# A fused attention and feed-forward kernel: a stored order of its pieces in place of a planner that orders them while the kernel is built

## The chip, the cores and the metric

The kernel runs on one core of one Trainium2 chip. The metric is device time in microseconds (us), taken over several runs; a verdict compares runs of two kernels on the same chip. The timed figure of a run is 1.7 to 2.1 us more than the span that the profile of the same run shows, so times and spans are compared each with its own kind.

## The reference, cut to what matters

Attention with a decay ("forgetting" attention) over 8 batches of 8 heads, 576 rows of 64, causal; its output feeds an RMS norm and a feed-forward network of 4608 tokens, 512 wide, 1536 hidden. Inputs and outputs are fp32; the kernel multiplies in bf16.

```python
def _attn_ref(q, k, v, f):                       # q, k, v: (8, 8, 576, 64), f: (8, 8, 576)
    scores = scale * np.matmul(q, k.transpose(0, 1, 3, 2))
    cum = np.cumsum(np.log(np.clip(f, 0.0001, 1.0)), axis=-1)
    decay = cum[:, :, :, None] - cum[:, :, None, :]
    scores = np.where(causal, -1000000000.0, scores + decay)
    ...                                           # softmax over the keys
    return np.matmul(attn, v)

def _moe_ref(x, w_gate, w_val, w_out, rms_g):    # x: (4608, 512)
    rms = np.sqrt(np.mean(x * x, axis=-1, keepdims=True) + 1e-06)
    xn = x / rms * rms_g
    g = xn @ w_gate
    silu = g * (1.0 / (1.0 + np.exp(-g)))
    return silu * (xn @ w_val) @ w_out
```

## The kernel before

The kernel does not write instructions straight down. It first collects 1564 *pieces*. A piece has a name, one engine, a function that writes its few instructions, the pieces it depends on, and the buffers that it takes from a pool (`acq`) or gives back (`rel`). Then a planner runs through them on a rough model of the engines, and their functions are called in the order that it yields. Each engine then takes its own instructions in that order, and semaphores hold it back: at 198 us, shown below, DVE stands at an `xn` whose input is late although a `ga` behind it has been ready since 196.2 us.

```python
class Plan:
    def run(self):                       # before: a greedy planner, cut
        ...
        while n_left:
            for e in self.ENGINES:
                c = [p for p in ready[e] if can(p, t)]      # ready, and its buffers free
                ...
                if e == "PE":
                    behind = a_done < self.lead + (a_total - self.lead) * min(1.0, f_done / (f_total * self.until))
                    first = "A" if behind else "F"          # attention or feed-forward
                    p = min(c, key=lambda p: (p.kind != first, p.prio))
                elif e == "SP" and t > MIX[0]:
                    ...
                else:
                    p = min(c + soon, key=lambda p: p.prio)
        ...
        return sorted(order, key=lambda p: p.start)
```

The names that matter below: `L` loads, `C` casts to bf16, `tr` transposes of q and k on TensorE and `keeptr` their copies out of PSUM, `sc` scores, `esc` the exponentials of scores on ScalarE, `msc` their causal masks on POOL, `val` the products with V, `xpo` the division by the softmax sum, `sq`, `ms`, `rs`, `xn` the norm, `xtr` (on TensorE) or `tx` (by DMA) the transposes of `xn`, `g` and `v…f` the gate and value matmuls of the feed-forward, `th` the tanh of the gate, `ga` and `hga` its products on DVE, `pj` the projection, `k4`, `sc4`, `exp4` the last 64-row block of keys, `wg`, `wv`, `wo` the weights. The first number is the batch (or, for the feed-forward, the group of tokens), the second the head pair, the row block or the hidden block.

There are only two PSUM buffers for scores, each given back by its exponential:

```python
    plan = Plan({"st": N_ST, "ld": N_LD, "pt": N_PT, "x": 2, "xn": N_XN, "xT": 3, "hT": 2, "th": 3, "ga": 2,
                 "ores": 3, "sc": 2, "po": 1, "ff": 3}, LEAD, UNTIL)
    ...
        def scores(visit):
            for p, (c0, blocks, _) in visit:
                sc = T["sc", b, p, c0] = ps_sc.tile([128, 2, 512], F32, name="sc", tag="sc")
                warm_up(sc[:, 0, :])
                ...                                     # the matmuls of the scores
        def exps(p, bank):
            ...
            nc.scalar.activation(T["pt", b, p][:, :, c0:c0 + n], T.pop(("sc", b, p, c0))[:, :, 0:n], ACT.Exp, scale=scale)
```

TensorE is kept busy with *fillers*: 128x128 matmuls of zeros.

```python
    def warm_up(ps):
        for _ in range(st.pop("fill", 0)):
            nc.tensor.matmul(ps[:, 0:128], lhsT=idle, rhs=idle, start=True, stop=True)
    ...
    with tc.manual_schedule():
        end = 1.3
        for p in plan.run():
            if p.eng == "PE":
                idle_for = p.start - end
                st["fill"] = FIRST if end < 2 else max(0, int((idle_for - 0.25) / FILL)) if p.start < WARM else 0
                end = p.end
            p.fn()
```

The softmax here doesn't subtract the row's maximum and nothing guards it: scores larger than these inputs give would overflow.

Of the kernel before, what the change touches and what calls it, by code (L numbers as in the profile page):

```python
# [19 lines left out]
NP = H // 2  # L20

LEAD, UNTIL = 30.0, 0.74
Q_AHEAD, V_AHEAD, T_AHEAD = 1.6, 0.9, 0.95
SPLIT, PE_TURN, PE_X = (0,), (0, 1, 2), (0, 1)
POOL_K, MIX = (), (55.0, 0.4)
S_SC, S_VAL, S_X, S_POOL = 3.0, 1.0, 2.0, 3.0
GROUPS = ((0, 256), (256, 512)) + tuple((a, a + 512) for a in range(512, B * S, 512))
ROWS, RUNS, HALF, TAIL, V4 = (1.2, 26, 64), (0.75, 46, 16), (0.9, 28, 32), (0.64, 24, 32), (0.34, 24, 16)
TURN, CAST, STORE = (0.6, 20, 64), (2.1, 32, 64), (0.78, 96, 8)
N_ST, N_LD, N_PT, N_XN = 10, 6, 4, 5  # L30
W_AFTER = ("Cq0.1", "Cq0.1", "Cq0.3", "Cqk0", "Ck1.0", "Cq1.0", "Ck1.1", "Cq1.1", "Sv1.0", "Sv1.1")
SPLIT_CAST = ({"k": "POOL", "q": "POOL"}, {"k": "POOL", "q": "POOL"}, {"k": "DVE", "q": "POOL"}, {"k": "DVE", "q": "POOL"})
TURNS = ((0, (0,)), (0, (1,)), (0, (2,)), (0, (3,)), (1, (0, 1)), (1, (2, 3)))
AFTER = (("tr0.10", "val0.6.0"), ("Cq0.2", "msc0.3.0"))
KEEP_K, SOON = ("ACT", "ACT", "DVE", "DVE"), 0.15
FILL, FIRST, WARM, COLD = 0.085, 48, 62.0, 1.15
CAST_ON, SV_ON, REST_P = {("q", 1, 2): "DVE", ("k", 1, 3): "DVE"}, {(1, 0): "DVE"}, 0.9
SV_PRIO, ST_SLACK = -0.7, 1.5
W_PRIO, WO_PRIO = (-1.5, -1.2, -1.1, -1.05), (-0.6, -0.55)
# [10 lines left out]
class Piece:  # L50


    __slots__ = ("name", "eng", "dur", "fn", "deps", "acq", "rel", "prio", "xfer", "kind",
                 "start", "end", "done", "nwait", "users", "ready", "seq", "got", "slack")

    def __init__(self, name, eng, dur, fn, deps, acq, rel, prio, xfer, kind):
        self.name, self.eng, self.dur, self.fn = name, eng, dur, fn
        self.deps = [d for d in deps if d is not None]
        self.acq, self.rel, self.prio, self.xfer, self.kind = acq, rel, prio, xfer, kind
        self.start = self.end = self.done = self.seq = None  # L60
        self.users, self.got, self.slack = [], {}, 0.0


class Plan:






    ENGINES = ("PE", "ACT", "DVE", "POOL", "SP")
    TO = {"PE": 0.20, "ACT": 0.07, "DVE": 0.07, "POOL": 0.08, "SP": 0.05}
    RING, LAND, LANES, BEGIN, SOFT = 128, 1.75, 8, 0.8, (0.3, 1.4)

    def __init__(self, pools, lead, until):
        self.pools = {k: [0.0] * n for k, n in pools.items()}
        self.pieces, self.lead, self.until, self.n_seq = [], lead, until, 0

    def add(self, name, eng, dur, fn, deps=(), acq=(), rel=(), prio=(0,), xfer=None, kind="", seq=False, slack=0.0):
        p = Piece(name, eng, dur, fn, deps, list(acq), list(rel), prio, xfer, kind)  # L80
        p.slack = slack
        self.pieces.append(p)
        if seq:
            p.seq, self.n_seq = self.n_seq, self.n_seq + 1
        return p

    def run(self):
        left = {}
        for p in self.pieces:
            p.nwait = len(p.deps)  # L90
            p.ready = 0.0
            for d in p.deps:
                d.users.append(p)
            for k in p.rel:
                left[k] = left.get(k, 0) + 1
        held, freed = {}, {}
        ready = {e: [] for e in self.ENGINES}
        free_at = dict.fromkeys(self.ENGINES, self.BEGIN)
        lanes = {q: [None] * self.LANES for q in (True, False)}
        n_dma = {True: 0, False: 0}  # L100
        for p in self.pieces:
            if not p.nwait:
                ready[p.eng].append(p)
        a_total = sum(p.dur for p in self.pieces if p.eng == "PE" and p.kind == "A")
        f_total = sum(p.dur for p in self.pieces if p.eng == "PE" and p.kind == "F")
        a_done = f_done = 0.0
        t, order = 0.0, []
        n_left, next_seq = len(self.pieces), 0
        ring = {e: [] for e in self.ENGINES}
        coming, full = [], {}  # L110
        never = float("inf")

        def free(pool, t):
            return sum(1 for f in self.pools[pool] if f <= t + 1e-9)

        def can(p, t):
            if p.ready > t + 1e-9 or p.seq not in (None, next_seq):
                return False
            if p.xfer is not None:
                q = p.eng == "POOL"  # L120
                last = lanes[q][n_dma[q] % self.LANES]
                if last is not None and (last.done is None or last.done > t + 1e-9):
                    return False
            need = {}
            p.got = {}
            for pool, key in p.acq:
                if key not in held:
                    if isinstance(pool, tuple):
                        pool = next((x for x in pool if free(x, t) > need.get(x, 0)), pool[0])
                    need[pool] = need.get(pool, 0) + 1  # L130
                    p.got[key] = pool
            return all(free(pool, t) >= n for pool, n in need.items())

        def finish(p):
            for key in p.rel:
                left[key] -= 1
                freed[key] = max(freed.get(key, 0.0), p.done + 0.08)
                if not left[key]:
                    pool, i = held[key]
                    self.pools[pool][i] = freed[key]  # L140
            for u in p.users:
                lat = 0.0 if u.eng == p.eng and p.xfer is None else self.TO[p.eng]
                u.ready = max(u.ready, p.done + (0.02 if p.xfer is not None else lat) + u.slack)
                u.nwait -= 1
                if not u.nwait:
                    ready[u.eng].append(u)

        def shares():
            busy = [e for e in ring if ring[e]]
            total = sum(ring[e][0][0].xfer[1] for e in busy)  # L150
            return {e: ring[e][0][0].xfer[1] / total for e in busy}

        def waiting(e):
            return sum(x[1] / x[0].xfer[0] * x[0].xfer[2] for x in ring[e])

        def dma_next():
            best = min((c[0] for c in coming), default=never)
            for e, s in shares().items():
                head = ring[e][0]
                best = min(best, dma_t[0] + head[1] / s)  # L160
                if e in full:
                    over = waiting(e) - self.RING
                    per = head[0].xfer[2] / head[0].xfer[0]
                    if over / per < head[1]:
                        best = min(best, dma_t[0] + max(0.0, over / per / s))
            return best

        def dma_to(t):
            while dma_t[0] < t - 1e-9:
                step = min(t, max(dma_next(), dma_t[0] + 1e-7))  # L170
                sh = shares()
                for e, s in sh.items():
                    ring[e][0][1] -= s * (step - dma_t[0])
                dma_t[0] = step
                for e in sh:
                    if ring[e][0][1] <= 1e-6:
                        p = ring[e].pop(0)[0]
                        p.done = step + self.LAND
                        finish(p)
                for c in [c for c in coming if c[0] <= step + 1e-9]:  # L180
                    coming.remove(c)
                    ring[c[1].eng].append([c[1], c[1].xfer[0]])
                    if c[1].eng in ("SP", "ACT") and waiting(c[1].eng) > self.RING:
                        full[c[1].eng] = c[1]
                        free_at[c[1].eng] = never
                for e in list(full):
                    if waiting(e) <= self.RING + 1e-6:
                        full.pop(e).end = free_at[e] = step

        dma_t = [0.0]  # L190
        while n_left:
            moved = False
            for e in self.ENGINES:
                if free_at[e] > t + 1e-9:
                    continue
                c = [p for p in ready[e] if can(p, t)]
                if not c:
                    continue
                soon = [p for p in ready[e] if t + 1e-9 < p.ready <= t + SOON and p.seq is None and can(p, p.ready)] if e in ("DVE", "ACT", "POOL") else []
                if e == "PE":  # L200
                    behind = a_done < self.lead + (a_total - self.lead) * min(1.0, f_done / (f_total * self.until))
                    first = "A" if behind else "F"
# [8 lines left out]
                else:  # L211
                    p = min(c + soon, key=lambda p: p.prio)
                    if p.ready > t + 1e-9:
                        continue
# [24 lines left out]
            if moved:  # L239
                continue  # L240
# [818 lines left out]
```

## Time and profile before

| | before |
|---|---|
| time, median of 3 runs | 390.03 us (389.24 to 391.62) |
| span of the profiled run | 391.9 us |
| TensorE busy by the page | 366.8 us (94%) |
| end of the first two token groups (12th tanh) | 62.1 us |
| from there to the end | 329.8 us |

The last two rows are read from the trace: the end of the twelfth tanh marks the point where the feed-forward's first two groups (512 tokens) have all their gates. They split the span into *start* and *rest*.

The first lines are from the page of the kernel before: the busy time of each engine; the span in 40 slices of 9.8 us with the busy tenths of TensorE, the granted clock in tenths; and the engines' shares of the chain that ended last.

```profile
span 391.9 us, 8390 instructions
PE 366.8 (94%) x3244; PEld 198.9 (51%) x3244; DVE 250.1 (64%) x460; ACT 217.2 (55%) x357; POOL 176.2 (45%) x281
PE   6778999789999996998979999999999999999996
PEclk9999999989999999999999999999999999999999
PE 64%; DMA 13%; SPq 8%; POOL 6%; issue 4%; ACT 3%; DVE 2%; POOLq 0%; ACTq 0%
```

TensorE bounds the kernel (94% busy, 64% of the chain that ended last), and after the start it is not full in five slices: two around 78 us, and those around 152, 181 and 201 us. The waits of TensorE, for the kernel before, give total time, times and the longest one in us:

```profile
PE sc L717 <- POOL K L708: 5.3, 3, 3.1
PE ff L952 <- DVE ga L961: 2.7, 2, 2.4
PE ff L845 <- DVE xn L818: 2.4, 1, 2.4
```

The timeline of the kernel before around the first stall: start, duration, engine, what it does, how often, and in brackets the idle time before it with what ended it.

```profile
76.03 3.96 DVE L818 SCALAR_TENSOR_TENSOR xn<-x,rs,rgb 128x512 bf16<-128x512 f32 x2 [0.52 <-POOL rs L814]
76.60 1.05 POOL L531 TENSOR_TENSOR Vs<-st,decT 128x512 bf16<-128x512 f32 x1
...
77.73 1.04 POOL L531 TENSOR_TENSOR Vs<-st,decT 128x512 bf16<-128x512 f32 x1
78.72 0.68 POOL L532 CAST Vs<-decT 128x8 bf16<-128x8 f32 x1
79.38 0.61 PE L845 MATMUL ff<-ident,xn 128*128 128x128 bf16 x4 [2.44 <-DVE xn L818]
```

Two `xn` normally take 1.5 us; here they took 3.96: the first one, 3.30 us long against a normal 0.75, lay across a row of POOL instructions. This `xn` is recorded from 76.03 us, before the first of the row at 76.60.

The timeline of the kernel before at the other three stalls:

```profile
148.74 2.63 POOL L524 CAST ld<-st 128x512 bf16<-128x512 f32 x3
151.33 0.85 POOL L708 COPY K<-QT 64x256 bf16<-64x256 bf16 x2
152.23 0.29 PE L717 MATMUL sc<-QT,K 128*128 128x64 bf16 x4 [3.12 <-POOL K L708]
...
177.46 0.84 POOL L708 COPY K<-QT 64x256 bf16<-64x256 bf16 x2 [5.07 <-DMA QT<-ld]
178.35 0.29 PE L717 MATMUL sc<-QT,K 128*128 128x64 bf16 x4 [1.48 <-POOL K L708]
...
198.15 1.62 DVE L818 SCALAR_TENSOR_TENSOR xn<-x,rs,rgb 128x512 bf16<-128x512 f32 x1 [1.78 <-POOL rs L814]
199.69 0.67 DVE L961 SCALAR_TENSOR_TENSOR ga<-th,ff 128x512 f32<-128x512 f32 x1
200.42 1.02 PE L952 MATMUL ff<-xT,wv 128*128 128x512 bf16 x4 [2.44 <-DVE ga L961]
```

One more view of the kernel before, ScalarE's timeline in the start, is needed later (the squares of the norm, `junk<-x`, and the exponentials of scores, one 128x1024 of which takes 1.0 us):

```profile
15.90 0.63 ACT L803 ACTIVATE junk<-x 128x512 bf16<-128x512 f32 x1
...
16.66 0.63 ACT L803 ACTIVATE junk<-x 128x512 bf16<-128x512 f32 x1
...
17.29 1.00 ACT L758 ACTIVATE PT<-sc 128x1024 bf16<-128x1024 f32 x1
19.02 1.94 ACT L758 ACTIVATE PT<-sc 128x1024 bf16<-128x1024 f32 x2 [0.72 <-PE sc L750]
21.75 1.02 ACT L758 ACTIVATE PT<-sc 128x1024 bf16<-128x1024 f32 x1 [0.79 <-PE sc L750]
...
24.86 1.02 ACT L758 ACTIVATE PT<-sc 128x1024 bf16<-128x1024 f32 x1
```

The exponential at 17.29 us is the fifth of the kernel and the last line the tenth: 7.6 us from start to start, about 1.5 us each.

### The profile page before, as it was taken

What the parts mean: (1) busy time and instruction counts of PE and PEld (TensorE: products, weight loads), DVE (VectorE), ACT (ScalarE), POOL (GpSimd) and SP (SyncE); (2) the same over time, 40 slices, a digit from 0 to 9 for tenths busy, and PEclk for the clock granted to TensorE, in tenths of its full rate; (3) what the DMA queues carried; (4) which work ended last, traced back from release to release, by engine and by line L of the source; (5) the groups of instructions that cost most, each with busy time, mean ns of one, the idle gap of its engine ahead of it and who ended that gap; (6) DMA issues with size and microseconds to landing.
All of it is one profiled execution on the core that took longest, in us unless ns stands there. A gap on an engine that the chain in (4) does not pass through costs nothing.

```text
span 391.9 us, 8390 instructions
## 1 busy us (share of the span) xinstructions
PE 366.8 (94%) x3244; PEld 198.9 (51%) x3244; DVE 250.1 (64%) x460; ACT 217.2 (55%) x357; POOL 176.2 (45%) x281
## 2 busy tenths in 40 slices
PE   6778999789999996998979999999999999999996
PEld 6457678445445542554534544445454544444444
DVE  6878767667776587436771688378627865843850
ACT  6585873746786585544735756464755453323321
POOL 6786647677486267547445816820321121001000
PEclk9999999989999999999999999999999999999999
DMA  9999999956697699699949969600230015002002
GB/s 206 207 264 215 213 254 221 227 133 107 135 219 157 135 201 208 98 192 207 180 98 227 240 116 174 145 26 2 48 122 2 0 38 132 3 27 80 2 1 107
DMA packets 144840, 52.61 MB, mean 134 GB/s; under 512 B 128220, under 2 KB 142304, under 8 KB 144800
## 3 DMA queue, kind: packets, MB, share of 16 engines
q1 hardware_dynamic: 136336, 38.82, 50.6%
q0 software_dynamic: 8384, 13.11, 14.5%
q8 instruction: 25, 0.41, 0.4%
q14 instruction: 15, 0.12, 0.1%
q10 hardware_dynamic: 80, 0.15, 0.1%
HBM read 37.90 MB, written 9.44 MB: 121 GB/s over the span
## 4 chain that ended last, share of the span: by engine, by line
PE 64%; DMA 13%; SPq 8%; POOL 6%; issue 4%; ACT 3%; DVE 2%; POOLq 0%; ACTq 0%
PE ff L952 33%; PE ff L978 21%; DMA st<-in_k_dram 4%; PE sc L750 4%; PE po L786 3%; DMA QK<-ld 3%; SPq L680 3%; SPq L495 3%; DMA wv<-in_moe_w_val_dram 2%; POOL ld L524 2%; PE ff L786 2%; DMA st<-in_q_dram 2%; DMA st<-in_v_dram 2%; ACT junk L803 1%; SPq L544 1%
## 5 line engine op out<-in xcount | busy, mean ns | idle before, releaser
L952 PE MATMUL ff<-xT,wv 128*128 128x512 bf16 (+1 forms) x480 | 111.0, 358 | 3.7 <-DVE ga L961 2.7
L758 ACT ACTIVATE PT<-sc 128x1024 bf16<-128x1024 f32 (+2 forms) x100 | 96.8, 991 | 31.0 <-PE sc L750 27.4
L961 DVE SCALAR_TENSOR_TENSOR ga<-th,ff 128x512 f32<-128x512 f32 x108 | 74.0, 685 | 60.0 <-ACT th L957 59.7
L952 PE MATMUL ff<-xT,wg 128*128 128x512 bf16 (+1 forms) x480 | 111.0, 358 | 0.1
L957 ACT ACTIVATE th<-ff 128x512 f32<-128x512 f32 x108 | 64.3, 595 | 65.7 <-PE ff L952 65.2
L978 PE MATMUL ff<-wo,hT 128*128 128x512 bf16 (+1 forms) x444 | 99.9, 377 | 0.0
L968 DVE SCALAR_TENSOR_TENSOR hT<-ga,ff 128x512 bf16<-128x512 f32 x108 | 74.2, 688 | 16.8 <-PE ff L952 7.6
L952 PEld LDWEIGHTS <-wv 128*128 128x128 bf16 x480 | 44.4, 98 | 47.5 <-issue 6.9
L952 PEld LDWEIGHTS <-wg 128*128 128x128 bf16 x480 | 45.2, 98 | 44.3 <-issue 1.7
L978 PEld LDWEIGHTS <-hT 128*128 128x128 bf16 x444 | 42.2, 99 | 47.0 <-issue 2.5
L766 POOL TENSOR_SCALAR_AFFINE_SELECT PT<-PT 128x1024 bf16<-128x1024 bf16 (+1 forms) x44 | 38.5, 886 | 47.4 <-ACT PT L758 32.8
L524 POOL CAST ld<-st 128x512 bf16<-128x512 f32 x68 | 42.7, 648 | 32.5 <-DMA QK<-ld 13.0
L983 ACT COPY ores<-ff 128x512 f32<-128x512 f32 (+1 forms) x37 | 21.2, 573 | 49.3 <-PE ff L978 47.8
L818 DVE SCALAR_TENSOR_TENSOR xn<-x,rs,rgb 128x512 bf16<-128x512 f32 x40 | 38.0, 994 | 5.5 <-POOL rs L814 5.4
L786 PEld LDWEIGHTS <-PT 128*128 128x128 bf16 x896 | 33.6, 98 | 10.6 <-POOL PT L766 1.5
L986 POOL DMA_DIRECT2D out_dram<-ores x32 | 18.3, 571 | 38.3 <-ACT ores L983 38.2
L531 POOL TENSOR_TENSOR Vs<-st,decT 128x512 bf16<-128x512 f32 x27 | 29.5, 1093 | 10.3 <-DMA st<-in_v_dram 5.3
L750 PE MATMUL sc<-QK 64*128 64x128 bf16 (+2 forms) x328 | 28.3, 269 | 2.1 <-DVE QK L633 2.1
L795 DVE RECIPROCAL rden<-po 128x5 f32<-128x5 f32 (+2 forms) x42 | 8.0, 191 | 31.7 <-PE po L786 30.7
L803 ACT ACTIVATE junk<-x 128x512 bf16<-128x512 f32 x40 | 25.1, 628 | 4.8 <-DVE x L796 4.1
L814 POOL TENSOR_TENSOR rs<-ms,mhalf 128x5 f32<-128x5 f32 (+2 forms) x9 | 10.0, 1108 | 34.4 <-DVE ms L809 34.3
L750 PEld LDWEIGHTS <-QK 64*128 64x128 bf16 x584 | 15.9, 94 | 18.1 <-issue 13.1
(84 smaller groups left out, 245.7 us busy)
## 6 DMA issues: line engine op xcount, KB each, us to landing
st<-in_k_dram SPq DMA_DIRECT2D x32, 256.0 KB, 5.0
st<-in_q_dram SPq DMA_DIRECT2D x32, 256.0 KB, 5.1
st<-in_v_dram SPq DMA_DIRECT2D x32, 256.0 KB, 4.9
out_dram<-ores POOLq DMA_DIRECT2D x32, 256.0 KB, 2.9
wo<-in_moe_w_out_dram POOLq DMA_DIRECT2D x2, 768.0 KB, 11.1
st<-in_q_dram SPq DMA_DIRECT2D x8, 128.0 KB, 4.9
st<-in_k_dram SPq DMA_DIRECT2D x8, 128.0 KB, 4.6
st<-in_v_dram SPq DMA_DIRECT2D x16, 64.0 KB, 4.1
```

The lines of the kernel that those rows point to most:

```text
L524: {"DVE": nc.vector.tensor_copy, "POOL": nc.gpsimd.tensor_copy, "ACT": nc.scalar.copy}[eng](o, x)
L531: e.tensor_tensor(Vs[i][:, j, :, 0:D], t, bcast(dj, D), ALU.mult)
L750: nc.tensor.matmul(sc[:, par, c:c + n], lhsT=k_cols(r, p, kj), rhs=q_cols(r, p, q0, n), start=True, stop=True)
L758: nc.scalar.activation(T["pt", b, p][:, :, c0:c0 + n], T.pop(("sc", b, p, c0))[:, :, 0:n], ACT.Exp, scale=scale)
L766: nc.gpsimd.affine_select(out=d, in_=d, pattern=[[0, m], [1, 128]], compare_op=ALU.is_ge, fill=0.0, base=0, channel_multiplier=-1)
L786: nc.tensor.matmul(T["po", b, hs][:, qm, m, :], lhsT=w, rhs=Vs[i][:, kj, h, :], start=(kj == 0), stop=(kj == qi))
L818: nc.vector.scalar_tensor_tensor(xn, in0=T["x", b][:, j, :], scalar=T["rs", b, js][:, j:j + 1], in1=rgb, op0=ALU.mult, op1=ALU.mult)
L952: nc.tensor.matmul(ps[:, c * w:c * w + w], lhsT=wt[:, dc, (fc + c) * 128:(fc + c + 1) * 128], rhs=T["xT", g][:, dc, 0:w], start=(dc == 0), ...
L957: nc.scalar.activation(t, T["pg", g, fc], ACT.Tanh, scale=0.5)
L961: nc.vector.scalar_tensor_tensor(a, in0=T.pop(("th", g, fc)), scalar=1.0, in1=T.pop(("pg", g, fc)), op0=ALU.add, op1=ALU.mult)
L968: nc.vector.scalar_tensor_tensor(o, in0=T.pop(("ga", g, fc)).rearrange("p (c t) -> p c t", t=w), scalar=0.5, in1=T.pop(("pv", g, fc)).rear ...
L978: nc.tensor.matmul(po, lhsT=T["hT", g][:, fc, j * 128:(j + 1) * 128], rhs=wo[:, fc, c0:c1], start=(fc == 0), stop=(fc == NFC - 1))
```

## The change

The planner is thrown out. In its place stands one string with the names of all 1564 pieces in the order in which they are to be written. By the change's own words, that order was found off chip by local search on a model of the kernel's run. A word `name*N` puts N fillers ahead of the piece; `name:ff` names the PSUM pool that a `val` takes. Pieces, shapes, engines and buffers stay; one small memset moves to an earlier POOL piece. Fillers go from 106 to 176; in both, 48 of them stand at the very start.

```diff
-LEAD, UNTIL = 30.0, 0.74
-Q_AHEAD, V_AHEAD, T_AHEAD = 1.6, 0.9, 0.95
+ORDER = """
+one lf ident Lk0.0 Lq0.1 rg identb clear Lk0.1 Lq0.0 Lq0.2 Lqk11 Lk0.2 clip turn_rg*48 keep_rgT Lqk00 Ck0.0 fetch_ln spread_rg*3 Lv0.0 Cq0.1 log scan
+Lv0.1 Cq0.0 Ck0.1 tr0.01*29 tr0.00 Cq0.2 Lk0.3 keeptr0.00.k keeptr0.00.q keeptr0.01.k expo Lqk01 keeptr0.01.q tr0.02*7 sc0.1.0 keeptr0.02.q Lv0.40
 ...
+Lq1.3 keeptr0.12.q keeptr0.10.k trt0 sq0.0 keeptrt0 sc0.3.512*1 esc0.3.512 ms0.0 rs0.0 keeptr0.12.k sc0.2.512*10 wv1 xn0.0 esc0.2.512 Sv0.3 wg2
 ... (the rest of the 1564 names is cut)
     def run(self):
-        left = {}
-        ... (the planner is cut)
-        return sorted(order, key=lambda p: p.start)
+        at = {p.name: p for p in self.pieces}
+        for word in ORDER.split():
+            word, _, fill = word.partition("*")
+            name, _, pool = word.partition(":")
+            p = at.pop(name)
+            for pools, key in p.acq:
+                p.got[key] = pools if isinstance(pools, str) else pool or pools[0]
+            yield p, int(fill or 0)
+        assert not at
 ...
     with tc.manual_schedule():
-        end = 1.3
-        for p in plan.run():
-            if p.eng == "PE":
-                idle_for = p.start - end
-                st["fill"] = FIRST if end < 2 else max(0, int((idle_for - 0.25) / FILL)) if p.start < WARM else 0
-                end = p.end
+        for p, fill in plan.run():
+            st["fill"] = fill
             p.fn()
```

## The prediction

> **What bounds the kernel now.** TensorE. The page says PE is busy 366.8 of 391.9 us, but its ends are modelled, so I counted matmul starts in the trace: a warm 128x512 matmul costs 0.216 us, a 65-column one 0.03 us, all useful ones together about 341 us. Of the other 50 us, 22 lie before 42 us (only 20 us of useful work is done by then), about 23 in gaps after it, 1.7 in half clock, the rest in the tail.
> - Start: loads saturate the DMA (windows: shares of 0.9 to 1.2 until 70 us), so work arrives late.
> - After 42 us the timeline shows four large PE stalls: ending at 79.4 us (xn transposes wait for a pair of xn instructions that took 4.0 us; 2.6 us), 152 and 178 us (last-block scores wait for K4, which waits for a DMA transpose; 3.3 and 1.6 us), 200 us (gate waits for rs, xn, transposed xT; 2.6 us). The clock record shows 3.4 us at half clock after the first. [...] The chain of waits runs through SP's queue and DMA landings before these stalls. From 205 us on gaps are small; the last 65 us are pure matmul.
>
> **What the change does.** The same 1564 pieces, shapes, engines and buffers; only order, some ordering edges and the filler count differ: 128 warming matmuls after the first 48, against 58. They run where PE would idle, so should cost nothing.
>
> **Costs by stretch.**
> - Start: the first transposes now need the third cast and fourth load instead of the second: 2 to 3 us later than 6.0 us. The fillers imply that the author's model sees many gaps of 0.4 to 2.7 us. By group 0's fifth gate (about 42 us) I expect the same time, within 2.5 us.
> - Stall 1: about 8 us of PE work now stands between batch 1's last values and its first xn transpose, where squares, rs and xn take about 7.5 us. Gain 2 to 4 us, clock included.
> - Stalls 2 and 3: K4's DMA transpose goes out 7 to 9 us of PE work before the scores that need it. Gain 3 to 5.
> - Stall 4: the last xT transpose goes out 4 us of PE work before the gate; landing takes about 3. Gain 1.5 to 2.6.
> - SP's bursts of transposes (1.2 us each) are now interleaved with loads.
> - New stalls: a fixed order has no slack for DMA jitter or slow DVE/POOL instructions; I allow 3 to 5 us.
> - Last 65 us: unchanged.
>
> Net: 390.0 - 12.5 (stalls and clock) + 4 (new stalls) - 2.5 (small gaps between 45 and 130 us) = 379 us. Range 371 to 386. Chances: faster by over 2% 0.72, within 2% 0.25, slower by over 2% 0.03.
>
> **What would show it.** PE waits on K4, xn and xT below 1 us each; no half clock at 79 us; group 0's gates at about the same time; a chain of waits with less SP queue and DMA, more PE; the same last 65 us.
>
> **What would make it wrong.** The start several us faster (then near 371), or slower through late first transposes and the out-of-turn load of batch 1's key tail; SP blocking behind a buffer that frees late, which holds all later loads; POOL, filled to 10 us in one stretch of batch 4, running late; DVE lengthened by POOL in new places.

What the 12.5 holds for the clock rests on the 3.4 us at half clock in the trace of before. In that stretch the starts of 128x512 matmuls lie 0.427 us apart instead of 0.216, so 3.4 us at half clock cost 1.7 us.

What the traces show of its other statements on the hardware: in the trace of before 128x512 matmuls start 0.216 us apart and 65-column ones 0.029 (medians), and the DMA share is 0.91 to 1.24 in each 10 us up to 70. A transpose by DMA occupies SP's queue for 1.22 us in the median of before; the transposes of `xn` landed after 2.8 us in before and 3.0 in after (medians; 2.3 to 5.8 us in before). The same old order had its second and third stall at 3.25 and 1.6 us in the trace of before and at 1.39 and 2.70 us in control's. In before, loads on SP stood 15.6 us in 14 waits, 3.0 us the longest, until a cast on POOL ended. And for DVE beside POOL there is the `xn` of 3.30 us above.

## The result

Ratios here and below are the mean time of one kernel's runs over the mean of the other's of the same rounds, so not quite the ratio of the medians that are quoted; brackets after a ratio hold its 95% interval.

| | before | after |
|---|---|---|
| time, median (lowest to highest) | 389.86 us (389.24 to 391.62) | 384.19 us (383.86 to 384.69) |
| ratio | | 0.9849 [0.9815, 0.9882] |
| span of the profile | 391.9 us | 382.2 us |
| end of the start (12th tanh) | 62.1 us | 66.1 us |
| rest | 329.8 us | 316.0 us |

The change made the kernel 1.5% faster in this first comparison, which is "same" at a threshold of 2%; repeated on another chip (`after_again` below) it was 2.1% faster, 0.9787 [0.9752, 0.9821], which is "unclear", since the interval takes in the threshold of 2%. The spans differ by more (9.7 us) than the times (5.7 us) because the profile of the kernel before had caught one of its slower runs: that run was timed at 393.63 us, above the four timed ones.

The page of the kernel after, the same lines:

```profile
span 382.2 us, 8426 instructions
PE 366.8 (96%) x3270; PEld 203.7 (53%) x3314; DVE 243.5 (64%) x460; ACT 215.1 (56%) x357; POOL 171.5 (45%) x281
PE   8768899989999999999999999999999999999996
PEclk9899999999999999999999999999999999999999
PE 88%; DVE 3%; ACT 3%; DMA 2%; issue 1%; POOL 1%; POOLq 0%; ACTq 0%
```

After the ninth slice TensorE is at nine tenths up to the tail, and the chain is TensorE at 88% where it was 64%. The two largest of TensorE's waits in the kernel after:

```profile
PE sc L235 <- ACT PT L628: 2.4, 2, 1.3
PE ff L235 <- DVE idle L245: 1.1, 1, 1.1
```

The waits for K, `ga` and `xn` that led the list before are gone from it. (The source lines are others in the new file: L235 are the fillers, L620 the scores, L811 the gate.) The two waits shown lie before 26 us, in the start. At the place of the old first stall the timeline of the kernel after reads:

```profile
78.81 4.89 DVE L688 SCALAR_TENSOR_TENSOR xn<-x,rs,rgb 128x512 bf16<-128x512 f32 x5
80.05 0.40 PE L715 MATMUL ff<-ident,xn 128*128 128x128 bf16 x4 [0.39 <-DVE xn L688]
84.09 0.38 PE L715 MATMUL ff<-ident,xn 128*128 128x128 bf16 x4 [0.60 <-DVE xT L722]
```

Five `xn` now take 4.89 us, about 1 us each, and TensorE waits 0.39 and 0.60 us instead of 2.44. Counted from matmul start to matmul start, less the usual time of a matmul, as the prediction counts, the largest gap after 60 us is 0.74 us. So the rest won 13.7 us and the start lost 4.0 us. Both had to be tested, because one pair of profiles of two kernels, one of them of a slow run, does not show which part of the change does what.

A part of what the start loses is seen on ScalarE. Its timeline in the kernel after (the same kinds of line, others left out):

```profile
19.05 1.02 ACT L628 ACTIVATE PT<-sc 128x1024 bf16<-128x1024 f32 x1 [1.45 <-PE sc L620]
20.56 0.63 ACT L673 ACTIVATE junk<-x 128x512 bf16<-128x512 f32 x1 [0.48 <-DVE x L666]
...
21.18 0.57 ACT L508 COPY QK<-ff 128x512 bf16<-128x512 bf16 x1
21.65 0.63 ACT L673 ACTIVATE junk<-x 128x512 bf16<-128x512 f32 x1
...
22.27 1.01 ACT L628 ACTIVATE PT<-sc 128x1024 bf16<-128x1024 f32 x1
23.18 0.58 ACT L508 COPY QK<-ff 128x512 bf16<-128x512 bf16 x1
24.42 1.02 ACT L628 ACTIVATE PT<-sc 128x1024 bf16<-128x1024 f32 x1 [0.66 <-PE sc L620]
26.59 1.94 ACT L628 ACTIVATE PT<-sc 128x1024 bf16<-128x1024 f32 x2 [1.14 <-PE sc L620]
28.88 1.05 ACT L628 ACTIVATE PT<-sc 128x1024 bf16<-128x1024 f32 x1
```

The fifth exponential starts at 19.05 us and the tenth at 28.88: 9.8 us for what took 7.6 us before (17.3 to 24.9), though the first ten are the same kinds in both kernels (all four head pairs of the first bank, all four of the second, two of the third). The rest of ScalarE's work between them is not the same: the kernel after has the squares and two copies here (2.3 us), the kernel before had the squares before its fifth exponential and a tanh here (0.5 us). Of the 2.3 us of difference 1.7 us is such work, and 0.6 us is longer waiting. And TensorE's timeline in the kernel after, over the same time:

```profile
20.81 0.39 PE L620 MATMUL sc<-QK 64*128 64x256 bf16 x4
...
21.66 0.40 PE L620 MATMUL sc<-QK 64*128 64x256 bf16 x4
23.34 0.72 PE L235 MATMUL sc<-idle 128*128 128x128 bf16 x10 [1.29 <-ACT PT L628]
23.99 0.39 PE L620 MATMUL sc<-QK 64*128 64x256 bf16 x4
25.50 0.72 PE L235 MATMUL sc<-idle 128*128 128x128 bf16 x10 [1.12 <-ACT PT L628]
```

Scores wait for a buffer until an exponential ends, then ten fillers run in that buffer, then the scores, then the next exponential.

### The profile page after: what moved, and what is told of

It reads as the page before. It is cut to its first block, busy times and chain, and to the rows that moved or that the text cites. A ratio compares the mean times of both kernels' runs of the same rounds, so it can differ in the third digit from the quotient of the medians.

```text
span 382.2 us, 8426 instructions
## 1 busy us (share of the span) xinstructions
PE 366.8 (96%) x3270; PEld 203.7 (53%) x3314; DVE 243.5 (64%) x460; ACT 215.1 (56%) x357; POOL 171.5 (45%) x281
## 4 chain that ended last, share of the span: by engine, by line
PE 88%; DVE 3%; ACT 3%; DMA 2%; issue 1%; POOL 1%; POOLq 0%; ACTq 0%
PE ff L811 49%; PE ff L837 23%; PE sc L620 6%; PE po L656 4%; PE ff L656 3%; DMA wg<-in_moe_w_gate_dram 2%; PE ff L235 2%; DVE xn L688 1%; ACT junk L673 1%; DVE x L666 1%; POOL PT L636 1%; ACT QK L513 1%; DVE QK L513 1%; PE ff L491 0%; ACT L271 0%
## 5 line engine op out<-in xcount | busy, mean ns | idle before, releaser
L628 ACT ACTIVATE PT<-sc 128x1024 bf16<-128x1024 f32 (+2 forms) x100 | 96.8, 990 | 28.4 <-PE sc L620 28.3
L811 PE MATMUL ff<-xT,wg 128*128 128x512 bf16 (+1 forms) x467 | 110.2, 357 | 1.9 <-DMA wg<-in_moe_w_gate_dram 1.0
L811 PE MATMUL ff<-xT,wv 128*128 128x512 bf16 (+1 forms) x464 | 109.7, 357 | 0.8
L837 PE MATMUL ff<-wo,hT 128*128 128x512 bf16 (+1 forms) x429 | 97.2, 373 | 0.7
L636 POOL TENSOR_SCALAR_AFFINE_SELECT PT<-PT 128x1024 bf16<-128x1024 bf16 (+1 forms) x44 | 37.2, 856 | 77.1 <-ACT PT L628 75.7
L811 PEld LDWEIGHTS <-wg 128*128 128x128 bf16 x480 | 44.7, 98 | 44.3 <-issue 1.7
L811 PEld LDWEIGHTS <-wv 128*128 128x128 bf16 x480 | 45.1, 98 | 42.4 <-issue 1.0
L412 POOL CAST ld<-st 128x512 bf16<-128x512 f32 x68 | 42.7, 651 | 23.6 <-DMA st<-in_q_dram 9.8
L688 DVE SCALAR_TENSOR_TENSOR xn<-x,rs,rgb 128x512 bf16<-128x512 f32 x40 | 33.9, 877 | 5.4 <-POOL rs L684 5.3
L845 POOL DMA_DIRECT2D out_dram<-ores x32 | 18.4, 576 | 39.6 <-ACT ores L842 39.6
L620 PE MATMUL sc<-QK 64*128 64x128 bf16 (+2 forms) x328 | 29.2, 273 | 1.1 <-DVE QK L508 1.0
L620 PEld LDWEIGHTS <-QK 64*128 64x128 bf16 x584 | 16.0, 95 | 18.3 <-issue 13.3
L656 PE MATMUL po<-Vs,PT 128*128 128x65 bf16 x521 | 22.3, 194 | 0.2 <-DVE Vs L420 0.2
L666 DVE TENSOR_TENSOR x<-po,rden 128x320 f32<-128x320 f32 (+2 forms) x39 | 18.6, 478 | 1.3
```

The source lines that it names most:

```text
L412: {"DVE": nc.vector.tensor_copy, "POOL": nc.gpsimd.tensor_copy, "ACT": nc.scalar.copy}[eng](o, x)
L620: nc.tensor.matmul(sc[:, par, c:c + n], lhsT=k_cols(r, p, kj), rhs=q_cols(r, p, q0, n), start=True, stop=True)
L636: nc.gpsimd.affine_select(out=d, in_=d, pattern=[[0, m], [1, 128]], compare_op=ALU.is_ge, fill=0.0, base=0, channel_multiplier=-1)
L656: nc.tensor.matmul(T["po", b, hs][:, qm, m, :], lhsT=w, rhs=Vs[i][:, kj, h, :], start=(kj == 0), stop=(kj == qi))
L688: nc.vector.scalar_tensor_tensor(xn, in0=T["x", b][:, j, :], scalar=T["rs", b, js][:, j:j + 1], in1=rgb, op0=ALU.mult, op1=ALU.mult)
L811: nc.tensor.matmul(ps[:, c * w:c * w + w], lhsT=wt[:, dc, (fc + c) * 128:(fc + c + 1) * 128], rhs=T["xT", g][:, dc, 0:w], start=(dc == 0), ...
```

## The experiments

Twelve kernels ran, in three calls on three chips; each call has its own runs of the kernel before (medians 391.72, 391.74 and 392.36 us). All gave correct results. In this table "5th" and "10th" are the starts of the fifth and tenth exponential, "half clock" is how long TensorE was granted half clock before 60 us; all are read from one trace each. That trace is of one run, not always a typical one: control's is of its fastest run (387.62 us), table_early's and old_rest's of their slowest (387.97 and 396.98).

| kernel | time, us | ratio to before | 5th | 10th | 12th tanh ends | rest | half clock |
|---|---|---|---|---|---|---|---|
| before | 389.86 | | 17.3 | 24.9 | 62.1 | 329.8 | 0 |
| after | 384.19 | 0.9849 | 19.0 | 28.9 | 66.1 | 316.0 | 3.4 |
| control | 390.31 | 0.9962 | 17.0 | 23.6 | 59.7 | 326.2 | 0 |
| old_start | 379.47 | 0.9708 | 18.1 | 24.3 | 61.5 | 315.8 | 6.8 |
| old_rest | 395.21 | 1.0069 | 19.0 | 28.9 | 65.5 | 329.8 | 3.4 |
| table_early | 384.47 | 0.9841 | 18.1 | 28.9 | 70.0 | 315.9 | 13.7 |
| after_again | 383.17 | 0.9787 | 19.0 | 29.9 | 67.0 | 315.6 | 6.8 |
| gate_first | 384.29 | 0.9799 | 19.8 | 30.4 | 66.8 | 315.6 | 10.2 |
| no_fill | 385.57 | 0.9838 | 19.5 | 28.9 | 68.0 | 315.7 | 23.9 |
| first_turn | 382.55 | 0.9762 | 17.5 | 28.3 | 65.5 | 314.9 | 6.8 |
| old_head | 384.69 | 0.9804 | 17.0 | 31.4 | 68.6 | 315.0 | 17.1 |
| free_fill | 383.65 | 0.9770 | 19.3 | 28.6 | 66.3 | 315.6 | 13.7 |
| start_mended | 382.78 | 0.9751 | 18.6 | 27.8 | 65.4 | 314.9 | 13.7 |
| old_start_ff | 382.09 | 0.9735 | 18.4 | 26.3 | 64.7 | 315.9 | 17.1 |

### Which part of the order does what

**control: the old order in the new form.** The order and the fillers that the old planner yields, stored in the new string. Instructions are the same on all engines but for the one memset that the change moved.

```diff
-ORDER = """one lf ident Lk0.0 Lq0.1 rg identb ... """
+ORDER = """lf one ident Lk0.0 clear fetch_ln Lq0.0 rg ... """   # what the planner yielded, all 1564
```

> The order that the kernel before works out, written as a stored order into the changed kernel; only one small memset on POOL stands earlier. Both theories: the same time as before (ratio 0.997 to 1.003), since storing the order does nothing by itself. Its profile is a second look at the old order. Theory (the first profile of before, 391.9 us, caught a run some 3 us longer than most, with the half clock after the stall at 79 us): this span is 388 to 389 us and the stalls for xn, K4 and xT after 50 us sum to 7 to 9 us. Rival (every run has them, and the profile is like the timed runs): the span is 391 to 392 and the four stalls sum to 10 us or more with a half-clock stretch near 79 us.

Measured 390.31 us (387.62 to 391.46), ratio 0.9962 [0.9911, 1.0014]. The form of storing costs and gains nothing that the interval shows; whatever the change does, the order does. The trace has the same kinds of stall as before: gaps ending at 76.9 (2.58 us), 146.6 (1.39) and 173.8 us (2.70), and 3.4 us of half clock after the last. With one of 0.65 us at 70.4 they sum to 7.3 us, as the theory of a slow first profile had it; the span of 385.9 us is shorter than either expected, because this profile is of control's fastest run.

**old_start: the old order for the first 290 pieces, then the new one.** The old order stands up to the scores `sc1.3.512` of batch 1 (about 55 us), then come all pieces not yet used, in the new order.

```diff
-one lf ident ... (the new order up to sc1.3.512)
+lf one ident ... (the old order up to sc1.3.512)
 ... (all pieces that are left, in the new order)
```

> Old order and fillers up to the last score visit of batch 1 (about 55 us), new order from there. Theory (the new order gains after 55 us and gives back about 3 us in the start): faster than the changed kernel by 2 to 3.5 us, near 381 us, ratio to before 0.974 to 0.981. Rival (the two parts hang together: the new rest is timed to the new start, and loads issued in the start decide it): 384 us or more, with new stalls between 55 and 90 us.

Measured 379.47 us (379.02 to 382.0), ratio 0.9708 [0.9663, 0.9754]: faster than both kernels, and by more than the theory's 0.974 to 0.981. The span of its profile is 377.3 us, and on its page no slice of TensorE between the start and the tail is under nine tenths. Its exponentials, in ScalarE's timeline of old_start, come almost without pause:

```profile
18.10 2.83 ACT L628 ACTIVATE PT<-sc 128x1024 bf16<-128x1024 f32 x3
21.16 1.02 ACT L628 ACTIVATE PT<-sc 128x1024 bf16<-128x1024 f32 x1 [0.23 <-PE sc L620]
...
24.27 1.02 ACT L628 ACTIVATE PT<-sc 128x1024 bf16<-128x1024 f32 x1
```

The tenth starts at 24.27 us, 4.6 us sooner than in the kernel after, though the fifth is only 0.95 us sooner. The new order of the rest keeps its whole gain behind the old start: 315.8 us.

**old_rest: the mirror image.** The new order for the 299 pieces up to `sc1.3.512`, then the rest in the old order.

```diff
 one lf ident ... (the new order up to sc1.3.512)
-... (the new order)
+... (all pieces that are left, in the old order)
```

> New order up to the last score visit of batch 1 (about 55 us), old order from there. Theory: slower than before by 2 to 3.5 us, 392 to 393.5 us, ratio 1.005 to 1.010, with the old waits for xn, K4 and xT back. Rival: within 1 us of before or of the changed kernel.

Measured 395.21 us (391.86 to 396.98), ratio 1.0069 [0.9997, 1.0141], within the theory's ratio though the interval takes in 1; rest 329.8 us, start 65.5 us, and old gaps are back (TensorE waits of 2.45 us ending at 82.1 and 2.85 us at 153.5). On this one chip the parts add up: against control's 390.31 us the new rest alone is worth 10.8 us (379.47) and the new start alone costs 4.9 us (395.21). Together that makes 384.4 us; the new order with one piece moved, the next kernel, took 384.47. That they agree to 0.1 us is luck, since old_rest's runs lie 5.1 us apart; the firmer figure for the new start is table_early less old_start, 5.0 us on the same chip.

**table_early: one load of ScalarE's table moved.** In the new order the `fetch` of the table for exponentials stands so late that the decays' own exponential loads it at 10.06 us, 1.28 us long, in the path of the start; in the kernel before it was loaded at 5.69 us, 2.16 us ahead of the decays' exponential at 7.85.

```diff
-... Cq0.1 log scan Lv0.1 ... Sv0.0 fetch msc0.0.0 ...
+... Cq0.1 log fetch scan Lv0.1 ... Sv0.0 msc0.0.0 ...
```

> The changed kernel with one move: the dummy Exp that fetches the activation table goes right behind the Ln on ACT, where ACT idles 3.5 us, as the old order has it. In the profile after, the table load of 1.28 us sits at 10.06 us, directly before the Exp of the decays, on the chain that ended last. Theory (the model behind the order counts the fetch as a piece of its own and does not know that any first Exp pays for it): that Exp starts 1.2 us earlier and the kernel is 0.8 to 1.3 us faster than the changed one, near 383.1 us. Rival (the start is bound by weight loads, group 0's first gate waits for its weights until 29.9 us): under 0.3 us.

Measured 384.47 us (383.88 to 387.97), ratio 0.9841 [0.9786, 0.9897], verdict unclear. The fifth exponential came 0.9 us sooner (18.1) and the tenth did not (28.9, as in the kernel after); but this trace, of the slowest run, had half clock from 23.4 to 37.0 us, so it does not tell whether the gain would have lasted. No gain in time is seen. The intervals of this ratio and of the kernel after on its own chip reach about 0.5% (2 us), so a gain of 0.8 to 1.3 us is neither shown nor ruled out. What the load costs is its 1.28 us: in the trace of the kernel after the next activation starts 1.29 us after the load began (10.06 to 11.35).

### Three suspects in the start

**after_again: the changed kernel once more**, unedited, so that these kernels have it on their own chip.

```diff
 (no edit: the changed kernel as it is)
```

> The changed kernel unaltered, as the base of the other three on the same chip. All theories: ratio to before 0.981 to 0.989. In its profile the last tanh of groups 0 and 1 should end at 65 to 67 us if the clock stays full from 16 us on, and from there to the end 316 us, as in the first look.

Measured 383.17 us (382.77 to 384.51), ratio 0.9787 [0.9752, 0.9821]. The start ended at 67.0 us and half clock was 6.8 us, where the first trace of the same program had 66.1 and 3.4: a microsecond in one trace's start is not a finding where the half clock differs.

**gate_first: the first gate weights ahead.** TensorE waits 0.97 us for the first gate weights at 29.9 us, because the new order issues three weight loads with `wg0` as the last.

```diff
-... sc0.3.0*8 wv0 tr0.10 esc0.3.0 ... wg1 ... sc0.0.512 wg0 Lq1.3 ...
+... sc0.3.0*8 wg0 tr0.10 esc0.3.0 ... wv0 ... sc0.0.512 wg1 Lq1.3 ...
```

> The changed kernel with the first weight loads in the order in which the gates need them: the first quarter of the gate weights now goes out at 14.9 us instead of 20.7 us, the other two move back one place. Theory (weights bind the start: the first gate stood 1.0 us waiting for them): the first tanh starts 0.8 to 1.2 us earlier, the kernel is 0.5 to 1.2 us faster than the changed one. Rival (ACT's exponentials bind up to there, and the batch 1 loads after): under 0.3 us.

Measured 384.29 us (383.05 to 384.45), ratio 0.9799 [0.976, 0.9838], against 0.9787 of after_again: no gain, so the rival held. The tenth exponential was no sooner (30.4 us).

**no_fill: no fillers after the first 48.** All `*N` are dropped except the first.

```diff
-... tr0.01*29 ... sc0.3.0*8 ... sc0.2.512*10 ... sc0.1.1024*10 ...
+... tr0.01 ... sc0.3.0 ... sc0.2.512 ... sc0.1.1024 ...
```

> The changed kernel without its 128 warming matmuls after the first 48. Theory (they run in idle time, and only those before the first transposes, 1.6 us on the chain that ended last, delay work): 0 to 0.7 us faster or equal when the clock stays full, but more runs with half-clock stretches in the first 50 us, which cost 1 to 4 us, so a wider spread and a median 0 to 2 us slower. Rival (the fillers themselves cost the start its 4 us): 2 to 4 us faster.

Measured 385.57 us (384.7 to 385.85), ratio 0.9838 [0.9806, 0.987]: 2.4 us slower than after_again by the medians. The trace shows 23.9 us of half clock before 60 us. The idea that the kernel would be 2 to 4 us faster without fillers falls; in sum they earn their place, and the half clock that came without them is the likely reason (mean granted clock 0.968 to 0.973 in its four runs, 0.991 to 1.0 in those of after_again). What fillers cost where they run after a wait is not separated here from what they save in clock.

**first_turn: the loads and casts of batch 0 back in turn**, so that the first transposes need the first two loads again; the 29 fillers ahead of the first transposes go too.

```diff
-Lk0.0 Lq0.1 ... Lk0.1 Lq0.0 ...   Ck0.0 ... Cq0.1 ... Cq0.0 Ck0.1 tr0.01*29 tr0.00
+Lk0.0 Lq0.0 ... Lk0.1 Lq0.1 ...   Ck0.0 ... Cq0.0 ... Ck0.1 Cq0.1 tr0.01 tr0.00
```

> The changed kernel with the first four loads and casts in the old order (k, q of the first half heads, then of the second), and without the 29 fillers before the first transpose. Theory (the late first transposes push everything of the start back): first transpose at 7.0 to 7.4 us instead of 8.75, first exponential 1 us or more earlier, kernel 0.8 to 2 us faster. Rival (the start is bound by the later loads and by POOL's casts, which hold the weight loads behind them): first exponential earlier, yet the last tanh of group 1 and the time within 0.5 us of the changed kernel.

That a weight load stands behind a cast on POOL is seen in table_early's chain of waits: a cast runs from 21.82 us, and `wg` follows at its end, 22.38.

Measured 382.55 us (381.81 to 382.81), ratio 0.9762 [0.973, 0.9793]. The first transposes started at 7.2 us (9.1 in after_again) and the fifth exponential at 17.5 (19.0). Both traces had 6.8 us of half clock at nearly the same place (from 23.2 and 24.2 us), and the 1.5 us lasted: the tenth exponential came at 28.3 (29.9) and the start ended at 65.5 (67.0). The time fell by 0.6 us in the medians and 1.0 in the means. The gain lay between what the two theories asked for, and the tenth exponential was still 3.4 us behind the kernel before. How much of it is the turn of the loads and how much the 29 fillers is not told apart.

### The head or the middle of the start

**old_head: the old order for the first 14 us only**, up to `val0.6.0`, then the new order.

```diff
-one lf ident ... (the new order up to val0.6.0)
+lf one ident ... (the old order up to val0.6.0)
 ... (all pieces that are left, in the new order)
```

> Old order up to the first values of batch 0 (about 14 us, with the first gate and value weights sent at 8 us), new order from there. Theory A (the start is lost in its first 14 us: late first transposes, the table load, weights behind the masks): the last tanh of groups 0 and 1 ends at 61 to 63.5 us and the time is near the old-start version's, ratio to before 0.969 to 0.976. Theory B (it is lost between 14 and 55 us, where scores, exponentials, casts and loads are ordered otherwise): that tanh ends at 65 us or later, ratio 0.977 to 0.985.

Measured 384.69 us (384.49 to 385.5), ratio 0.9804 [0.9777, 0.9832]. The fifth exponential starts at 17.0 us, as early as in control, and yet the tenth starts at 31.4 and the start ends at 68.6. ScalarE's timeline of old_head shows it, with one line of TensorE's:

```profile
16.96 1.02 ACT L628 ACTIVATE PT<-sc 128x1024 bf16<-128x1024 f32 x1 [4.43 <-PE sc L620]
...
20.35 1.03 PE L503 MATMUL ff<-ident,ld 128*128 128x128 bf16 x8 [2.46 <-POOL ld L412]
...
23.15 1.02 ACT L628 ACTIVATE PT<-sc 128x1024 bf16<-128x1024 f32 x1 [3.47 <-PE sc L620]
...
28.91 1.94 ACT L628 ACTIVATE PT<-sc 128x1024 bf16<-128x1024 f32 x2 [1.86 <-PE sc L620]
31.39 1.02 ACT L628 ACTIVATE PT<-sc 128x1024 bf16<-128x1024 f32 x1
```

ScalarE waits for scores in front of nearly every exponential, and the first of these waits stands behind transposes that wait 2.46 us for a cast on POOL. The old head alone does not bring the old start back. But TensorE had half clock from 16.1 to 33.2 us, over this whole stretch, so the order is not tested alone. An estimate of the clock's part: old_start_ff below has old_start's order, 10.2 us more half clock, and ended its start 3.2 us later. With that taken off, old_head's start would end at 65.4 us, still 3.9 us behind old_start's. By this estimate most of the loss does lie past the first 14 us; what the seam itself costs is open.

**free_fill: no fillers ahead of scores and of one `val`**, so that none of them can hold a score buffer's turn (176 fillers become 124).

```diff
-... sc0.2.0*5 ... sc0.3.0*8 ... val0.2.0*16 ... sc0.3.512*1 ... sc0.2.512*10 ... sc0.1.1024*10 ...
+... sc0.2.0 ... sc0.3.0 ... val0.2.0 ... sc0.3.512 ... sc0.2.512 ... sc0.1.1024 ...
```

> The changed kernel without the 52 warming matmuls that stand before score pieces and before the first values in the single values buffer. A filler writes the PSUM buffer of the piece it precedes, so where that piece waits for the buffer (the scores at 23.3 and 25.5 us wait for an exponential to free it) the fillers run after the wait, not in it. Theory (such fillers add their own 3 to 4 us to the chain of the start): 1 to 3 us faster than the changed kernel, last tanh of group 1 at 63.5 to 66 us. Rival (loads and casts bind there, and the clock needs the fillers): within 0.7 us or slower, with longer half-clock stretches before 50 us.

Measured 383.65 us (382.62 to 384.04), ratio 0.977 [0.9741, 0.9799]: no clear gain, against 0.9787 of after_again, as the rival had it. Half clock rose to 13.7 us. The trace does show the fillers' part: between the fifth and the tenth exponential ScalarE waited 0.8 us for scores, where after_again, with as much half clock there (5.9 and 5.7 us), waited 2.6, and the tenth came 9.3 us after the fifth instead of 10.9. So the fillers did hold the scores up, and what was won there did not reach the time.

**start_mended: all mends of the head together**: first_turn, table_early, the gate weights ahead, and no fillers on scores and values (95 fillers left).

```diff
-Lk0.0 Lq0.1 ... Lk0.1 Lq0.0 ... log scan ... msc0.1.0 ... wv0 ... wg1 ... wg0 ... fetch ... sc0.2.512*10
+Lk0.0 Lq0.0 ... Lk0.1 Lq0.1 ... log fetch scan ... wg0 wv0 msc0.1.0 ... wg1 ... sc0.2.512
```

> The changed kernel with all mends of its start at once: first loads and casts in the old order, the table fetch behind the Ln, the first gate and value weights sent before the first masks on POOL, no fillers before scores. Theory A (these causes together are the start's loss): the last tanh of group 1 ends at 60 to 63 us, ratio to before 0.967 to 0.975. Theory B (the rest of the start's order binds): 64 us or later, ratio 0.976 or more.

Measured 382.78 us (381.09 to 383.79), ratio 0.9751 [0.9706, 0.9795]. The start ended at 65.4 us, not near control's 59.7, and the time is at best 1 us below that of the changed kernel. That speaks against theory A, but does not settle it: this trace had 13.7 us of half clock, and the four runs lie in the order of their clocks (381.09 us at 0.986, 382.26 and 383.30 at 0.982, 383.79 at 0.978), while old_start's runs had 0.991 to 1.0. What these mends would give at full clock was not measured.

**old_start_ff: the best kernel without fillers on scores and values** (106 fillers become 66).

```diff
 (old_start, with the old order's first 290 pieces)
-... sc0.0.0*2 ... val0.0.0*8 ... val0.6.0*4 ... sc0.0.512*16 ... sc0.2.512*3 ... sc0.0.384*7 ...
+... sc0.0.0 ... val0.0.0 ... val0.6.0 ... sc0.0.512 ... sc0.2.512 ... sc0.0.384 ...
```

> The old-start version (old order to 55 us, new order after) without the 40 fillers before scores and in the single values buffer. If fillers on a busy buffer cost their own time: 0.3 to 1.5 us faster than the old-start version, ratio to before 0.966 to 0.970. If the clock needs them more: ratio 0.971 to 0.977, and half-clock stretches in the first 50 us longer than the 6.8 us seen there.

Measured 382.09 us (381.52 to 382.68), ratio 0.9735 [0.9707, 0.9762], where old_start had 0.9708 [0.9663, 0.9754] on another chip. It is not better, so old_start stays the best. Its trace has 17.1 us of half clock, against 6.8 in old_start.

### What stays argued

Shown: the loss lies in the order of the first 299 pieces (old_start against table_early on one chip, 5.0 us). Half clock is not what makes it, since old_start had 6.8 us of it, more than the kernel after, and ended its start 4.6 us sooner. About 1.5 us of it in the trace goes with the turn of the first loads and the 29 fillers (first_turn).

Not shown: where the rest is lost, and how. The kernels that were to divide it (no_fill, old_head, free_fill, start_mended) all drew 13.7 to 23.9 us of half clock, so none of them shows its order at full clock. Three readings of the traces remain.

- A held buffer. The order scores `sc0.0.512` early, at 20.8 us, but puts its exponential `esc0.0.512` behind those of `sc0.3.512`, `sc0.2.512` and `sc0.1.1024`; it starts at about 27.5 us, as the second of the pair at 26.59. So one of only two score buffers is held for 7 us, and the others take turns on the second, 2.2 us apart, where one exponential takes 1.0. The old order has no such pair. As a main cause this is weak: free_fill and start_mended hold the buffer too (5.5 us in free_fill), and there ScalarE waited 0.8 and 0.7 us for scores between the fifth and tenth exponential, where the kernel before waited 1.5.
- The fillers in that turn (0.65 us each time, from 23.34 to the scores at 23.99). free_fill shows that they lengthen the waits, and not that the time gains without them.
- Moved work. The squares and copies that ScalarE does between the fifth and tenth exponential, 1.7 us more work (less a tanh) than in the kernel before, are most of the 2.3 us of difference there. So these two landmarks do not enclose equal work, and part of what looks like a loss after the fifth was work put off before it.

The direct tests, `esc0.0.512` or the squares moved up in the new order, were not run.

## Why the prediction was right or wrong

**The time.** 379 us was predicted, with a range of 371 to 386; 384.19 us came, inside the range and 5.2 us above the middle. The chance of 0.72 for more than 2% faster was too high: the kernel lies at the border, 1.5% faster in one comparison and 2.1% in the other.

**The step that failed: "By group 0's fifth gate (about 42 us) I expect the same time, within 2.5 us."** By that mark (the third gate piece; its tanh comes at 41.1 us before and 44.0 after) it was 2.9 us later than in the profile of before and 5.4 us later than in control (38.6). By the end of the first two groups it was 4.0 and 6.4 us later. In time, the new start costs about 5 us (5.0 by table_early less old_start, 4.9 by old_rest). The prediction saw the late first transposes (8.7 us instead of 6.0, as written) and trusted that they would be caught up. They were one part of it: first_turn won 1.5 us of the start back, 0.6 us of the time. The larger part lies in other pieces of the start, which the prediction did not look at one by one; which of them, the runs leave open.

**The gain after the start: mechanism right, sum right by luck.** The prediction took 12.5 us for stalls and clock, 2.5 us for small gaps, and gave back 4 us for new stalls: 11 us. The rest gained 13.7 us against the profile of before (329.8 to 316.0) and 10.2 against control's (326.2 to 316.0), profiles of a slow and a fast run of the old order; in time, 10.8 us on one chip. The terms:

- Stalls and clock: the trace of before holds 2.6 + 0.65 + 3.25 + 1.6 + 2.6 us of gaps and 1.7 us for 3.4 us of half clock, 12.4 us together. The trace of after holds none of these. In control they are 2.58 + 0.65 + 1.39 + 2.70 + 1.7 = 9.0 us, so the term depends on which run is profiled.
- New stalls: 4 us was allowed; the largest gap after 60 us is 0.74 us. "A fixed order has no slack" was wrong here: the rest took 314.9 to 316.0 us in all eleven traces that had the new order there.
- Small gaps: 13.7 less 12.4 leaves 1.3 us, where 2.5 was taken.
- Last 65 us unchanged: right. From the end of the 84th tanh to the end it was 76.2 us before and 76.1 after.

**A detail that was wrong: the stall at 200 us.** The prediction said that the gate waited for rs, xn and the transposed xT. It was value matmuls that waited, and for a free PSUM buffer: DVE, in its fixed order, stood at an `xn` (1.78 us waiting for `rs` on POOL, then 1.62 us long) ahead of the `ga` that frees the buffer. The list of waits names `ga`. Also, only the stall at 178 us was a late DMA transpose, as the prediction had both; at 152 us POOL itself stood at three casts.

**"They run where PE would idle, so should cost nothing" (the fillers).** Right in sum: without them the kernel is 2.4 us slower. But the trace shows that they do not always run where TensorE would idle: written to a buffer that is waited for, they run after the wait.

**The clock.** The first stall's half clock is gone, as predicted. That the length of the stall made it is not shown: in the trace of before the clock was halved at 79 us after a stall of 2.6 us, and was not at 152 us after one of 3.25 us (see the last section). New drops came in the start, which the prediction did not foresee: 3.4 us in the kernel after, 6.8 us in its repetition.

**What it costs in the end.** The best kernel is old_start, the old start with the new rest: 379.47 us, 2.9% faster than before on the same chip (391.72), which is near where the prediction's sum would have landed had the start been equal.

## What to carry to other kernels

An order found by search on a model is only as good as the model's weakest stretch: compare old and new stretch by stretch at landmarks in the trace, not by total time, and splice the better stretches (here 379.5 us, against 384.5 for the new order with one piece moved and 391.7 for the old, on the same chip). When a variant is to test the order alone, compare the granted clock first: four variants here changed the order or the fillers and the clock with it, and so left the cause open. And take a second profile of the kernel before counting its stalls, since one profile may show a slow run (here 3.25 us of stall at one place in one trace and 1.4 in the next).

## What the traces show of the clock, of DVE beside POOL, of the table load and of fillers

- The clock. In the kernel before it fell to half at 79.36 us, for 3.41 us, after 2.82 us between two matmul starts; it stayed full at 152.23 us, after 3.50 us, and at 200.42 us, after 2.82 us. In the kernel after it fell at 12.76 us, for 3.41 us, and in the 3.4 us before, with 22 matmuls, no gap between matmul starts was over 1.25 us; it stayed full at 23.34 us, after 1.55 us. So the clock stayed full after the longest of these gaps, and fell after the shortest. These two traces give no rule for when it falls. Before 60 us the stretches of half clock lasted 3.4, 6.8, 10.2, 13.7, 17.1 and 23.9 us in sum per trace, all near multiples of 3.4; and the same program had 3.4 us in one trace and 6.8 in another.
- DVE beside POOL. One `xn` of 0.75 us took 3.30 us while POOL ran four instructions in a row (1.05, 0.22, 1.04 and 0.68 us), and was recorded as the earlier of the two. The next longest `xn` of the two traces took 1.83 us, across two POOL instructions of 0.68 and 0.62 us and the issue of a store of 0.59 us.
- The table load. It is 1.28 us long. In these traces it begins 0.02 us after the instruction before it ends, and the next activation starts 1.29 to 1.30 us after the load began (10.06 to 11.35 in after, 5.69 to 6.99 in before).
- Fillers. Those written to a buffer that is still in use run after the wait and so delay what follows: ten of them took 0.65 us after waits of 1.29 and 1.12 us, and ScalarE's waits for scores fell from 2.6 to 0.8 us without them (after_again, free_fill).
